# The first weight's scale in front of the first rows, and four pieces decoded without order edges

## The chip, the cores and the metric

The kernel runs on one core of a Trainium2 chip. The metric is device time in microseconds (us) of one execution. Five engines run their own instruction queues and meet at semaphores: PE (TensorE, matrix products), DVE (VectorE), ACT (ScalarE), POOL (GpSimd) and SP (SyncE, which here only starts DMA transfers).

## What is computed

Eight batches of an approximate attention (landmarks, with six Newton steps for an inverse) over q, k, v of 8 heads x 576 tokens x 64, then a two-dimensional Fourier mix, a normalisation and a feed-forward of two matrices:

```python
X = np.fft.fft(np.fft.fft(x, axis=1), axis=2)
u = x + np.real(X)
un = (u - mu) / np.sqrt(var + 1e-06)
ch = np.maximum(un @ w_ch1, 0.0) @ w_ch2
return u + ch
```

x is the attention's output, 8 x 576 rows of 512. `w_ch1` is 512 x 2048 and `w_ch2` 2048 x 512, both float64. The feed-forward is most of the arithmetic.

## The kernel before

All matrix products that matter run as three float16 products of high and low halves (`mm3`). Work is written as Python threads, which a small planner interleaves: `attention`/`tokens`, `landmarks`, `values`, `mix` and `norm` for one batch after the other, `weights` for the two matrices, and `mlp` for the feed-forward. The planner keeps an estimated clock `self.now`, adds estimated durations, and takes at each moment the first thread by priority that isn't waiting. The order in which it emits PE's instructions is PE's order. The order on DVE, ACT and SP is made by the framework's scheduler from the dependencies; the planner adds edges for it (`Timed.emit`): where `A.late` or `V.late` is set to a time, the instruction must stand behind the last instruction on that engine whose estimated start isn't later than that time. Where a loaded piece lands late by the estimate, its decoding so stays behind work that can start earlier.

The weights come as float64 bits in 16 pieces each of 128 x 512 numbers, 0 to 15 for `w_ch1` and 16 to 31 for `w_ch2`. Each piece goes through these steps:

- `prepare`: ACT makes the exponent and upper bits from the high word (`row<-w` or `row<-big` in the trace).
- decoding: the low bits by DVE (even pieces, a TENSOR_SCALAR) or ACT (odd pieces, from a byte), joined by DVE (`w<-row,w`).
- `squares`: PE multiplies the piece with itself into `gram` (four 128 x 128 products, `acc<-w`), for the matrix's norm.
- `scale`, once for each matrix: DVE takes the diagonal (`wd`) and its sum (`wm`), PE adds it over the partitions (product with `ones`), DVE bounds it (`wp_e`), POOL takes the power -1/2 (`wp_r`), DVE writes the scale `wsc`.
- `halve`: ACT and DVE write the scaled piece as high and low float16 halves (`w<-w,wsc`).

No product of the feed-forward can start before its piece is halved. In the kernel before, `squares` lag the decoding by two pieces, and the first scale comes after piece 17.

`norm` normalises finished rows (DVE `row<-u,mv,r`, with POOL's power `r`), and for the first four row tiles transposes them on PE (`at<-ident,row`) and splits them into `unT` (ACT high, DVE low). `mlp` takes two row tiles as a chunk: for each pair of pieces 24 products `h<-unT,w` into one of two PSUM banks, a relu by ACT (high) and DVE (low), and, a little later, 12 products `acc<-w,h` into the chunk's two accumulators, which DVE adds to `u` when the chunk is done (`u<-acc`). Relus of the second chunk's first two pairs go to tiles named `u`.

As long as `self.spare` is there (until the second matrix's first product), the planner fills its own estimated gaps on PE with idle products of `ones16` and `idle`, 128 x 256.

Of the kernel before, what the change touches and what calls it, by code (L numbers as in the profile page):

```python
# [10 lines left out]
F32 = mybir.dt.float32  # L11
# [7 lines left out]
P = 128  # L19
H, S, D, LM, DM, DF = 8, 576, 64, 32, 512, 2048  # L20
NF = DF // P
# [12 lines left out]
AHEAD, PREP, EARLY = 1, 4, 2  # L34
# [124 lines left out]
class Kernel:  # L159
# [80 lines left out]
    def mm(self, out, a, b, start=True, stop=True, share=1.0):  # L240
        self.there[out.name] = self.now
        self.now += share * (1.0e-3 if a.dtype == F32 else 0.42e-3) * math.prod(b.shape[1:])
        self.nc.tensor.matmul(out, a, b, start=start, stop=stop, skip_group_check=True)  # L243

    def tr(self, out, a, ident):
        self.there[out.name] = self.now
        self.now += 0.11
        self.nc.tensor.transpose(out, a, ident)  # L248
# [26 lines left out]
    def weights(self):  # L275
        nc = self.nc
        V, A = self.V, self.A
        whole = self.whole
        slots = [[t[:, OFF + 512 * i : OFF + 512 * i + 512] for i in range(NF)] for t in whole]
        upper = [[t.bitcast(BF16).rearrange("p (m x) -> p m x", x=2)[:, :, 1] for t in ss] for ss in slots]  # L280
        hl = [[t[:, 512 * i : 512 * i + 512].bitcast(F16).rearrange("p (y m) -> p y m", y=2) for i in range(NF)] for t in whole]
        self.w1s = [t.rearrange("p y (c f) -> p y c f", c=KT) for t in hl[0]]
        self.w2s = hl[1]
        sc = self.cp.tile([P, 3], F32, name="wsc")
        pieces = [(w, f) for w in range(2) for f in range(NF)]
        mags = []

        def prepare(i):


            mag = self.row(512)
            top = self.wraw[i].rearrange("p (m x) -> p m x", x=2)[:, :, 1].bitcast(F32)
            A.late = self.raw_there[i]
            A.activation(mag, top, AF.Prelu, scale=2.0**-112, alpha=-(2.0**32))
            mags.append(mag)

        def squares(i):

            w, f = pieces[i]
            for c in range(KT):  # L300
                x = upper[w][f][:, P * c : P * c + P]
                self.mm(self.gram[:, P * w : P * w + P], x, x, i == 0 and c == 0, f == NF - 1 and c == KT - 1)

        es = []

        def scale(w):

            dg, a2 = self.small(P, "wd"), self.small(1, "wm2")
            V.tensor_tensor(dg, self.gram[:, P * w : P * w + P], self.ident, ALU.mult)
            V.tensor_reduce(a2, dg, AX.X, ALU.add)  # L310
            yield self.till(a2, banks=1)
            ps = self.psum()
            self.mm(ps[:, 0:1], self.ones, a2)
            e, r = self.small(1, f"wp{w}_e"), self.small(1, f"wp{w}_r")
            V.tensor_scalar(e, ps[:, 0:1], 2.0**-120, 2.0**126, ALU.max, ALU.min)
            self.G.tensor_tensor(r, e, self.mhalf[:, 0:1], ALU.pow)
            V.tensor_scalar(r.bitcast(I32), r.bitcast(I32), 0x7F800000, None, ALU.bitwise_and)
            V.reciprocal(e, r)
            es.append(e)
            V.tensor_scalar(sc[:, w : w + 1], r, (2.0**12, 2.0**14)[w], None, ALU.mult)  # L320

        def halve():
            w, f = pieces[sum(self.split_w)]
            self.split(hl[w][f][:, 0], hl[w][f][:, 1], slots[w][f], sc[:, w : w + 1])
            self.split_w[w] = f + 1

        for i, (w, f) in enumerate(pieces):
            while len(mags) < min(2 * NF, i + 1 + PREP):
                j = len(mags)
                while len(self.wraw) < min(2 * NF, j + 1 + AHEAD):  # L330
                    self.raw()
                if self.raw_there[j] > self.now:
                    if j > i:
                        break
                    yield self.raw_there[j] - self.now
                    continue
                prepare(j)
            low = self.wraw[i].rearrange("p (m x) -> p m x", x=2)[:, :, 0]
            x, dst = mags[i].bitcast(I32), slots[w][f].bitcast(I32)
            (A if i % 2 else V).late = self.raw_there[i]  # L340
            if i % 2 == 0:
                V.tensor_scalar(dst, low, 29, None, ALU.logical_shift_right)
            else:
                byte = self.wraw[i].bitcast(mybir.dt.uint8).rearrange("p (m x) -> p m x", x=8)[:, :, 3]
                A.activation(dst, byte, AF.Copy, scale=2.0**-5, bias=-0.484375)
            V.scalar_tensor_tensor(dst, x, 3, dst, ALU.logical_shift_left, ALU.bitwise_or)
            if i > 1:
                squares(i - 2)
            self.decoded = i + 1
            if self.decoded == 2 * NF:  # L350
                self.load(1)
            yield max(0.0, max(self.V.free, self.G.free) - self.now - WT)
            if i == NF + 1:
                yield from scale(0)
            for _ in range(PACE if es else 0):
                if self.split_w[0] < NF:
                    halve()
                    yield max(0.0, max(self.V.free, self.G.free) - self.now - WT)
        squares(2 * NF - 2)
        yield 0.0  # L360
        squares(2 * NF - 1)
        yield from scale(1)
        V.tensor_scalar(sc[:, 2:3], es[0], 2.0**-25, es[1], ALU.mult, ALU.mult)
        self.inv2 = sc[:, 2:3]
        while sum(self.split_w) < 2 * NF:
            halve()
            yield max(0.0, max(self.V.free, self.A.free) - self.now - WT)
# [52 lines left out]
    def tokens(self, b, st):  # L420

        nc, mm, mm3, tr, sm, split = self.nc, self.mm, self.mm3, self.tr, self.sm, self.split
        V, A = self.V, self.A
        self.load(b)
# [424 lines left out]
    def norm(self, b, uts):  # L849
        nc, V = self.nc, self.V  # L850
        n = len(uts)
# [29 lines left out]
        for j, ut in enumerate(uts):  # L881
            i = self.ntile
# [7 lines left out]
                )  # L890
            unT = self.unT[-1]
            at = P * (i % TCH)
            if i < 2 * TCH:
                yield self.till(uns[j], banks=1) + (LATER if i >= TCH else 0.0)
                ps = self.psum()
                for c in range(KT):
                    self.tr(ps[:, P * c : P * c + P], uns[j][:, P * c : P * c + P], self.ident)
                self.split(*(unT[:, y, :, at : at + P] for y in range(2)), ps.rearrange("p (c t) -> p c t", c=KT), 1.0)
                self.ready.append(self.now + self.till(unT))
                yield 0.0  # L900
                continue
# [89 lines left out]
    def run(self):  # L991
# [1 line left out]

        self.ntile, self.utiles, self.unT, self.ready = 0, [], [], []
        self.ulive, self.ufree, self.first_done, self.seconds, self.folded = 0, [], 0, 0, -1
        self.split_w, self.decoded = [0, 0], 0
        self.threads = []
        self.spawn(self.attention(), 1)
        self.spawn(self.weights(), 2)
# [85 lines left out]
```

## Time and profile before

| | us |
|---|---|
| median of 3 runs | 994.53 |
| lowest, highest | 993.15, 995.64 |
| the profiled execution | 993.68 |
| its span, first to last instruction | 991.9 |
| PE busy | 955.5 |
| DVE busy | 593.3 |
| ACT busy | 319.4 |
| POOL busy | 119.0 |

The profiled execution is 1.8 us longer than its span. Busy time of PE counts idle products too. In the views a tile's name stands without its buffer number, and as most DVE and ACT instructions go through one helper (L138), groups are told apart by their tiles. A wait is put down to the engine whose semaphore came last.

### The profile page before, as it was taken

The numbers are of one execution on the slowest core, as the hardware profiler recorded it, in microseconds if no ns is written. First come the engines' busy times: TensorE is split into PE (matmuls) and PEld (weight loads), VectorE is DVE, ScalarE is ACT, GpSimd is POOL, SyncE is SP. The second block draws the span as 40 slices with busy tenths as digits, with TensorE's granted clock in tenths as the row PEclk, the third lists the DMA queues.
The fourth block names the chain that finished last, engine by engine and source line by source line (L and its number), as shares of the span: only waits on it lengthen the run. The fifth ranks groups of instructions, "written<-read, shape, count | busy, mean of one in ns | idle before, by whom it ended". The sixth has DMA issues, their size and how long they took to land.

```text
span 991.9 us, 20749 instructions
## 1 busy us (share of the span) xinstructions
PE 955.5 (96%) x8700; PEld 664.2 (67%) x8700; DVE 593.3 (60%) x1593; ACT 319.4 (32%) x652; POOL 119.0 (12%) x124
## 2 busy tenths in 40 slices
PE   6869999899999999999999999999999999999998
PEld 4648656667666777676666776676766777666665
DVE  7989797796467635396467736784634835141111
ACT  5559653243214322143214322432213412120110
POOL 0000000023021301032012301150110401010000
PEclk8889999999999999999999999999999999999999
DMA  9854204135121511025112321134111301020000
GB/s 332 292 212 150 65 2 172 37 59 154 49 44 42 149 55 23 22 58 154 44 44 42 99 104 43 23 61 172 22 33 33 52 1 42 16 40 22 1 22 22
DMA packets 97774, 74.66 MB, mean 75 GB/s; under 512 B 68112, under 2 KB 86544, under 8 KB 97552
## 3 DMA queue, kind: packets, MB, share of 16 engines
q1 hardware_dynamic: 97680, 73.34, 25.6%
q8 instruction: 68, 1.11, 0.5%
q14 instruction: 26, 0.21, 0.1%
HBM read 48.02 MB, written 9.44 MB: 58 GB/s over the span
## 4 chain that ended last, share of the span: by engine, by line
PE 86%; DVE 9%; DMA 2%; ACT 2%; issue 1%; POOL 0%; SPq 0%; DVEq 0%; ACTq 0%; POOLq 0%
PE h L243 36%; PE acc L243 35%; PE at L243 14%; DVE w L138 2%; DVE u L138 1%; DVE lm L138 1%; DVE mid L138 1%; DVE row L138 1%; DMA big<-k_dram 1%; PE at L248 1%; DMA big<-v_dram 1%; ACT w L138 0%; DMA out_dram<-u 0%; ACT row L138 0%; ACT mid L138 0%
## 5 line engine op out<-in xcount | busy, mean ns | idle before, releaser
L243 PE MATMUL h<-unT,w 128*128 128x256 f16 x3456 | 411.2, 273 | 3.8 <-DMA unT<-row 1.7
L243 PEld LDWEIGHTS <-w 128*128 128x128 f16 (+1 forms) x3584 | 344.9, 99 | 79.9 <-DVE w L138 7.3
L243 PE MATMUL acc<-w,h 128*128 128x512 f16 x1632 | 381.6, 380 | 2.7 <-DVE w L138 2.2
L243 PEld LDWEIGHTS <-h 128*128 128x128 f16 x1632 | 157.2, 99 | 162.6 <-issue 6.3
L138 DVE SCALAR_TENSOR_TENSOR h<-h 128x512 f16<-128x512 f32 x136 | 93.6, 688 | 224.8 <-ACT h L138 224.6
L138 ACT ACTIVATE h<-h 128x512 f16<-128x512 f32 x136 | 80.9, 595 | 321.8 <-PE h L243 315.7
L138 POOL TENSOR_TENSOR r<-ve,mhalf 128x2 f32<-128x2 f32 (+1 forms) x20 | 13.3, 667 | 476.6 <-DVE ve L138 472.2
L138 POOL TENSOR_TENSOR mid<-mid 128x640 f16<-128x640 f32 (+2 forms) x36 | 48.7, 1365 | 161.1 <-ACT mid L138 123.7
L138 DVE TENSOR_REDUCE lm<-big 128x32 f32<-128x576 f32 (+1 forms) x48 | 44.5, 940 | 2.8 <-DMA big<-k_dram 2.5
L243 PEld LDWEIGHTS <-big 128*128 128x128 f16 (+1 forms) x864 | 40.1, 103 | 8.1 <-issue 1.9
L138 ACT CAST row<-row 128x512 f16<-128x512 f32 (+1 forms) x40 | 20.8, 552 | 63.9 <-DVE row L138 63.9
L138 POOL TENSOR_TENSOR row<-row 128x512 f16<-128x512 f32 (+1 forms) x33 | 35.4, 1089 | 39.6 <-ACT row L138 37.7
L243 PEld LDWEIGHTS <-mid 64*128 64x128 f16 (+1 forms) x624 | 29.3, 95 | 14.8 <-issue 8.2
L138 DVE SCALAR_TENSOR_TENSOR u<-at,scw,w 128x128 f32<-128x128 f32 (+3 forms) x105 | 33.8, 389 | 5.8 <-PE at L243 4.1
L138 DVE SCALAR_TENSOR_TENSOR u<-acc,wsc,u 128x512 f32<-128x512 f32 x36 | 26.9, 748 | 12.3 <-PE acc L243 12.0
L138 DVE SCALAR_TENSOR_TENSOR w<-at,scw,w 128x262 f32<-128x262 f32 (+1 forms) x42 | 19.1, 485 | 25.2 <-ACT w L138 25.2
L243 PE MATMUL at<-mid,big 128*128 128x262 f16 (+1 forms) x288 | 32.6, 282 | 0.0
L138 DVE TENSOR_TENSOR E<-at,mask 128x256 f32<-128x256 f32 x48 | 20.1, 419 | 17.9 <-PE at L243 17.9
L243 PEld LDWEIGHTS at<-RE,E 128*128 128x128 f32 x192 | 26.6, 194 | 5.0 <-DVE big L138 1.6
L243 PE MATMUL at<-RE,E 128*128 128x64 f32 (+1 forms) x192 | 29.0, 275 | 0.2 <-DVE RE L138 0.2
L138 DVE SCALAR_TENSOR_TENSOR big<-big,aq_r 128x1024 f16<-128x1024 f32 (+1 forms) x32 | 26.8, 868 | 3.5 <-ACT big L138 3.5
L138 DVE TENSOR_TENSOR mid<-mid 128x256 f32<-128x256 f32 (+2 forms) x52 | 28.6, 584 | 0.0
(179 smaller groups left out, 897.8 us busy)
## 6 DMA issues: line engine op xcount, KB each, us to landing
w<-w_dram SPq DMA_DIRECT2D x22, 512.0 KB, 6.8
big<-v_dram SPq DMA_DIRECT2D x16, 640.0 KB, 9.5
big<-q_dram SPq DMA_DIRECT2D x16, 584.0 KB, 6.7
big<-k_dram SPq DMA_DIRECT2D x16, 576.0 KB, 5.4
out_dram<-u SPq DMA_DIRECT2D x36, 256.0 KB, 2.0
big<-w_dram SPq DMA_DIRECT2D x10, 512.0 KB, 6.5
t<-t_dram SPq DMA_DIRECT2D x1, 1048.0 KB, 10.7
unT<-row SPq DMA_TRANSPOSE x64, 2.4
```

What stands on the lines that cost most here:

```text
L138: ins = call(out, *args, **kw)
L243: self.nc.tensor.matmul(out, a, b, start=start, stop=stop, skip_group_check=True)
L248: self.nc.tensor.transpose(out, a, ident)
```

## The change

`squares(14)`, `squares(15)` and `scale(0)` are now emitted right behind the decoding of piece 15. 24 idle products (`warm`) stand in front of `squares(15)` and 8 behind the scale's product with `ones`; that product now uses one of `mlp`'s two banks (`h`). `norm` holds its transposes until this product has been emitted (`self.scaled`). As soon as `es` is filled, the halving of the first matrix runs beside the decoding of the second, so it begins two pieces earlier. For pieces 28 to 31 `late` is 0, so that no order edge is added.

```diff
--- before.py
+++ after.py
@@ -242,6 +242,10 @@
         self.now += share * (1.0e-3 if a.dtype == F32 else 0.42e-3) * math.prod(b.shape[1:])
         self.nc.tensor.matmul(out, a, b, start=start, stop=stop, skip_group_check=True)
 
+    def warm(self, n):
+        for _ in range(n):
+            self.nc.tensor.matmul(self.spare[:, 0:256], self.ones16, self.idle, start=True, stop=True, skip_group_check=True)
+
     def tr(self, out, a, ident):
         self.there[out.name] = self.now
         self.now += 0.11
@@ -290,13 +294,15 @@
 
             mag = self.row(512)
             top = self.wraw[i].rearrange("p (m x) -> p m x", x=2)[:, :, 1].bitcast(F32)
-            A.late = self.raw_there[i]
+            A.late = self.raw_there[i] if i < 2 * NF - PREP else 0.0
             A.activation(mag, top, AF.Prelu, scale=2.0**-112, alpha=-(2.0**32))
             mags.append(mag)
 
         def squares(i):
 
             w, f = pieces[i]
+            if i == NF - 1:
+                self.warm(24)
             for c in range(KT):
                 x = upper[w][f][:, P * c : P * c + P]
                 self.mm(self.gram[:, P * w : P * w + P], x, x, i == 0 and c == 0, f == NF - 1 and c == KT - 1)
@@ -308,9 +314,12 @@
             dg, a2 = self.small(P, "wd"), self.small(1, "wm2")
             V.tensor_tensor(dg, self.gram[:, P * w : P * w + P], self.ident, ALU.mult)
             V.tensor_reduce(a2, dg, AX.X, ALU.add)
-            yield self.till(a2, banks=1)
-            ps = self.psum()
+            yield self.till(a2, banks=1) if w else max(0.0, self.there[a2.name] - self.now)
+            ps = self.psum() if w else self.ps_h.tile([P, 512], F32, name="h")
             self.mm(ps[:, 0:1], self.ones, a2)
+            if w == 0:
+                self.warm(8)
+            self.scaled = True
             e, r = self.small(1, f"wp{w}_e"), self.small(1, f"wp{w}_r")
             V.tensor_scalar(e, ps[:, 0:1], 2.0**-120, 2.0**126, ALU.max, ALU.min)
             self.G.tensor_tensor(r, e, self.mhalf[:, 0:1], ALU.pow)
@@ -337,20 +346,23 @@
                 prepare(j)
             low = self.wraw[i].rearrange("p (m x) -> p m x", x=2)[:, :, 0]
             x, dst = mags[i].bitcast(I32), slots[w][f].bitcast(I32)
-            (A if i % 2 else V).late = self.raw_there[i]
+            (A if i % 2 else V).late = self.raw_there[i] if i < 2 * NF - PREP else 0.0
             if i % 2 == 0:
                 V.tensor_scalar(dst, low, 29, None, ALU.logical_shift_right)
             else:
                 byte = self.wraw[i].bitcast(mybir.dt.uint8).rearrange("p (m x) -> p m x", x=8)[:, :, 3]
                 A.activation(dst, byte, AF.Copy, scale=2.0**-5, bias=-0.484375)
             V.scalar_tensor_tensor(dst, x, 3, dst, ALU.logical_shift_left, ALU.bitwise_or)
-            if i > 1:
+            if i > 1 and not NF <= i < NF + 2:
                 squares(i - 2)
             self.decoded = i + 1
             if self.decoded == 2 * NF:
                 self.load(1)
             yield max(0.0, max(self.V.free, self.G.free) - self.now - WT)
-            if i == NF + 1:
+            if i == NF - 1:
+                squares(NF - 2)
+                yield 0.0
+                squares(NF - 1)
                 yield from scale(0)
             for _ in range(PACE if es else 0):
                 if self.split_w[0] < NF:
@@ -890,6 +902,8 @@
                 )
             unT = self.unT[-1]
             at = P * (i % TCH)
+            while not self.scaled:
+                yield 0.1
             if i < 2 * TCH:
                 yield self.till(uns[j], banks=1) + (LATER if i >= TCH else 0.0)
                 ps = self.psum()
@@ -993,7 +1007,7 @@
 
         self.ntile, self.utiles, self.unT, self.ready = 0, [], [], []
         self.ulive, self.ufree, self.first_done, self.seconds, self.folded = 0, [], 0, 0, -1
-        self.split_w, self.decoded = [0, 0], 0
+        self.split_w, self.decoded, self.scaled = [0, 0], 0, False
         self.threads = []
         self.spawn(self.attention(), 1)
         self.spawn(self.weights(), 2)
```

The planner's clock changes with it, and so does the order of everything behind. PE has 26 idle products more in all (156 instead of 130 of that shape) and the same other products; their order is the same before this place and again, with few differences, from the end of the third batch on.

On PE, at the first weight's scale: `acc_109` are squares, `acc_108` the idle products, `wm` the scale's sum. Before:

```order
L243 MATMUL at<-mid,big 128x262
L243 LDWEIGHTS ones_102
L243 MATMUL acc_108<-idle,ones_102 128x256
L243 LDWEIGHTS ones_102
L243 MATMUL acc_108<-idle,ones_102 128x256
L243 MATMUL at<-wm_1022,ones 128x1
L243 LDWEIGHTS mid
L243 MATMUL at<-Wx,mid 128x4x32
```

And now:

```order
L243 MATMUL acc_109<-w_73 128x128
L243 LDWEIGHTS ones_102
L243 MATMUL acc_108<-idle,ones_102 128x256
L243 LDWEIGHTS ones_102
L243 MATMUL acc_108<-idle,ones_102 128x256
L243 MATMUL h<-wm_999,ones 128x1
L247 LDWEIGHTS ones_102
L247 MATMUL acc_108<-idle,ones_102 128x256
```

Before, the scale's product stood behind the eight transposes of the first rows and the twelve products `at<-mid,big` of the next tile; now it stands behind the squares, and the seven other idle products, the transposes and those twelve products follow it. The 24 idle products stand ahead of the four squares whose last is this piece's first row.

On DVE, at the end of the decoding (`w_74<-row,w_74` joins a piece of the second matrix, `u<-h,u` is the relu of the second chunk's first pairs, `wd` begins the second scale). Before:

```order
L138 TENSOR_SCALAR w_74<-big 128x512
L138 SCALAR_TENSOR_TENSOR w_74<-row,w_74 128x512
L138 SCALAR_TENSOR_TENSOR h<-h 128x512
L138 SCALAR_TENSOR_TENSOR u<-h,u 128x512
L138 SCALAR_TENSOR_TENSOR w_74<-row,w_74 128x512
L138 TENSOR_TENSOR wd<-acc_109,ident 128x128
```

And now:

```order
L138 SCALAR_TENSOR_TENSOR u<-at,scw,row 64x128 x2
L138 SCALAR_TENSOR_TENSOR h<-h 128x512
L138 SCALAR_TENSOR_TENSOR w_74<-row,w_74 128x512
L138 TENSOR_SCALAR w_74<-big 128x512
L138 SCALAR_TENSOR_TENSOR w_74<-row,w_74 128x512 x2
L138 SCALAR_TENSOR_TENSOR u<-h,u 128x512 x2
L138 TENSOR_TENSOR wd<-acc_109,ident 128x128
```

The last pieces are joined ahead of both relus, and the second relu, which stood behind the second scale, is ahead of it. ACT's order moved in the same way. The writes `u<-at` of the first batch's third tile stand right ahead of the relu `h<-h`; before, they stood ten rows higher.

On DVE, in the second batch (`mid<-at,mid` and `row<-at,row` split the transposes, the `mid<-mid` are the folds, `u<-acc` adds a finished accumulator). Before:

```order
L138 SCALAR_TENSOR_TENSOR u<-acc_1671,wsc,u 128x512
L138 RECIPROCAL asum<-asum 128x16
L138 TENSOR_REDUCE asum<-row 128x4
L138 SCALAR_TENSOR_TENSOR u<-acc_1672,wsc,u 128x512
L138 TENSOR_SCALAR asum<-asum 128x4
L138 TENSOR_TENSOR E<-at,mask 128x256
```

And now, the first `u<-acc` being some 13 rows higher:

```order
L138 TENSOR_TENSOR E<-at,mask 128x256
L138 TENSOR_TENSOR mid<-mid 128x256 x2
L138 TENSOR_TENSOR mid<-mid 128x512
L138 TENSOR_TENSOR RE<-RE,at 128x2x32
L138 TENSOR_TENSOR mid<-mid 128x512
L138 SCALAR_TENSOR_TENSOR u<-acc_1694,wsc,u 128x512
```

The second `u<-acc` moved from ahead of the splits to behind the last fold. On PE, 84 products `acc` now stand ahead of the second batch's transposes `at<-ident,mid` of its attention weights, where 99 stood before; behind these transposes follow the first chunk's last products and 24 products of the second chunk, whose sixth to twelfth go to the accumulator that this `u<-acc` empties.

## Rows read from the trace of the kernel before

**Rows 1.** The page's first part, PE's and the other engines' busy time, share of the span and instructions.

```profile
PE 955.5 (96%) x8700; PEld 664.2 (67%) x8700; DVE 593.3 (60%) x1593; ACT 319.4 (32%) x652; POOL 119.0 (12%) x124
```

**Rows 2.** Busy time by stage (windows). After the stretch's bounds in us stand its length, then busy time and instructions of PE, PE's weight loads, DVE, ACT and POOL, then PE's granted clock (1.00 is full speed, 2.4 GHz), the share of the DMA engines and GB/s.

```profile
62.69:82.07 19.38, 15.63 (x123) 12.57 (x123) 14.68 (x41) 11.64 (x23) 1.96 (x3) 0.74 0.25 84
71.47:82.07 10.60, 9.34 (x79) 7.57 (x75) 8.59 (x25) 9.42 (x19) 0.70 (x1) 0.84 0.17 51
82.07:105.38 23.31, 22.49 (x237) 19.86 (x235) 23.20 (x43) 19.65 (x34) 0.00 (x0) 1.00 0.59 194
105.38:111.42 6.04, 5.28 (x55) 4.66 (x54) 2.44 (x8) 2.31 (x4) 0.55 (x1) 1.00 0.13 42
112.77:153.68 40.91, 37.03 (x368) 20.64 (x366) 36.83 (x104) 22.87 (x47) 2.49 (x3) 0.96 0.06 18
153.68:210.00 56.32, 53.31 (x494) 36.17 (x493) 43.12 (x115) 18.04 (x37) 2.11 (x5) 1.00 0.32 97
260.00:992.00 732.00, 726.47 (x6383) 499.84 (x6381) 382.46 (x1017) 189.63 (x389) 98.48 (x97) 1.00 0.19 50
```

**Rows 3.** PE's timeline, first weight's last squares to the first products of the feed-forward. Columns: start and length in us, engine, line, operation, output<-inputs, shape, count, and in brackets the idle time before it and who ended it.

```profile
59.14 0.27 PE L243 MATMUL acc<-idle,ones 128*128 128x256 bf16 x1
62.18 0.40 PE L243 MATMUL acc<-w 128*128 128x128 bf16 x4 [2.77 <-DVE w L138]
...
64.84 1.94 PE L248 MATMUL at<-ident,row 128*128 128x128 f32 x8 [2.15 <-DVE row L138]
66.57 2.83 PE L243 MATMUL at<-mid,big 128*128 128x262 f16 x12
...
69.62 0.43 PE L243 MATMUL at<-wm,ones 128*128 128x1 f32 x2
...
72.42 0.39 PE L243 MATMUL h<-unT,w 128*128 128x256 f16 x2 [0.84 <-ACT w L138]
...
77.53 1.36 PE L243 MATMUL acc<-idle,ones 128*128 128x256 bf16 x11
78.73 1.47 PE L243 MATMUL h<-unT,w 128*128 128x256 f16 x12
```

**Rows 4.** The same window view as in rows 2, single microseconds; the column behind the engines is the granted clock.

```profile
63.00:64.00 1.00, 0.00 (x0) 0.00 (x0) 0.97 (x5) 0.00 (x0) 0.39 (x1) 0.63 0.38 61
69.00:70.00 1.00, 1.00 (x7) 0.86 (x6) 0.00 (x0) 0.48 (x1) 0.00 (x0) 0.50 0.00 0
```

**Rows 5.** Timelines of DVE and POOL, the first weight's scale and the two pairs of normalised rows (columns as in rows 3).

```profile
63.57 0.28 DVE L138 TENSOR_REDUCE wm<-wd 128x1 f32<-128x128 f32 x1
...
64.14 1.00 DVE L138 TENSOR_SCALAR row<-u,mv,r 128x512 f32<-128x512 f32 x2
...
70.08 0.16 DVE L138 TENSOR_SCALAR wp_e<-at 128x1 f32<-128x1 f32 x1 [1.94 <-PE at L243]
...
70.32 0.56 POOL L138 TENSOR_TENSOR wp_r<-wp_e,mhalf 128x1 f32<-128x1 f32 x1 [6.93 <-DVE wp_e L138]
...
71.47 0.14 DVE L138 TENSOR_SCALAR wsc<-wp_r 128x1 f32<-128x1 f32 x1
...
82.07 1.00 DVE L138 TENSOR_SCALAR row<-u,mv,r 128x512 f32<-128x512 f32 x2
```

**Rows 6.** Timelines of ACT, DVE and PE: ACT's first copy for `unT`, and the end of the decoding.

```profile
65.96 0.60 ACT L138 ACTIVATE unT<-at 128x512 f16<-128x512 f32 x1 [5.00 <-PE at L248]
...
105.96 0.60 ACT L138 ACTIVATE u<-h 128x512 f16<-128x512 f32 x1 [2.72 <-PE h L243]
...
106.45 0.67 ACT L138 ACTIVATE row<-big 128x512 f32<-128x512 f32 x1
...
106.59 0.69 DVE L138 SCALAR_TENSOR_TENSOR u<-h,u 128x512 f16<-128x512 f32 x1 [1.12 <-ACT u L138]
...
107.71 0.69 DVE L138 SCALAR_TENSOR_TENSOR w<-row,w 128x512 int32<-128x512 int32 x1 [0.43 <-ACT w L138]
...
108.46 0.41 PE L243 MATMUL acc<-w 128*128 128x128 bf16 x4 [0.77 <-DVE w L138]
```

**Rows 7.** Timelines of DVE and PE behind the second weight's scale: its `wsc`, the second matrix's first products, and PE's waits up to 210 us.

```profile
111.42 0.13 DVE L138 TENSOR_SCALAR wsc<-wp_r 128x1 f32<-128x1 f32 x1
...
112.77 10.91 PE L243 MATMUL acc<-w,mid 128*128 128x512 f16 x48
...
126.78 3.59 PE L243 MATMUL acc<-w,h 128*128 128x512 f16 x11 [2.23 <-DVE w L138]
...
150.47 0.81 PE L243 MATMUL acc<-w,u 128*128 128x512 f16 x3 [1.37 <-DVE u L138]
...
150.63 0.73 DVE L138 SCALAR_TENSOR_TENSOR u<-acc,wsc,u 128x512 f32<-128x512 f32 x1
...
153.79 1.46 PE L243 MATMUL acc<-w,u 128*128 128x512 f16 x6
...
158.56 0.69 DVE L138 TENSOR_TENSOR mid<-mid 128x512 f16<-128x512 f32 x1
...
187.29 0.49 PE L243 MATMUL at<-Wx,mid 64*128 64x128 f16 x11 [0.76 <-DVE w L138]
...
192.33 2.03 PE L243 MATMUL h<-unT,w 128*128 128x256 f16 x17 [1.75 <-DMA unT<-row]
...
207.28 1.46 PE L243 MATMUL acc<-w,h 128*128 128x512 f16 x6 [0.50 <-DVE u L138]
```

## The prediction

> **What bounds the kernel now.** I read the page's busy line first, then busy time by stage, then PE's timeline where it stands still, then the queues of DVE and ACT there. PE is busy 96% of the span [rows 1], and from 260 us on 726.5 of 732 us [rows 2]: nothing can be won there. The change sits where PE waits. In 62.7 to 82.1 us PE works 15.6 of 19.4 us and its granted clock averages 0.74; in 82.1 to 105.4 us DVE works 23.2 of 23.3 us, so that stretch is DVE's; from 112.8 to 153.7 us PE stands still for 3.9 of 40.9 us [rows 2]. PE waits 2.77 us for piece 15, then 2.15 us for the first rows [rows 3]; behind these gaps the clock goes to 0.5, half speed, and is there still at 69 to 70 us [rows 4]. The first product of the feed-forward starts at 72.42 [rows 3], because the scale `wsc` comes at 71.47 [rows 5], although its sum `wm` was there at 63.85 [rows 5]: PE's product with it is queued behind eight transposes and twelve products and ends at 70.05 [rows 3].
>
> **The idle products.** Eleven run from 77.53 to 78.73, 0.109 us each [rows 3]. 24 take 2.6 us and lie in the gap from 59.4 to 62.18 [rows 3]: nothing unless they start over 0.1 us later, and then that much. Eight more, 0.9 us, lie between the scale's product (about 64.1) and the first transposes (65.0). With PE busy from 59 to 66 I take the clock to stay full; at half speed the eight transposes and twelve products took from 64.84 to 69.40 [rows 3], 4.6 us, at full speed I take half of it. If the clock falls all the same, that half, 2.3 us, isn't won (the third rival).
>
> **The scale.** `wm` ends at 63.85; the product takes 0.3, `wp_e` follows at 64.2, POOL's power 0.24 us later for 0.56 us [rows 5], and `wsc` is there at 65.6, 5.9 us earlier. The two row normalisations stand behind `wp_e` and slip by 0.1 to 0.4 us. ACT has no work until 65.96 [rows 6] and takes the first split in that hole; its two copies for `unT` come behind it, and DVE's second part of `unT` ends at about 68.3, near to where it did. So `unT` becomes what is late, and the first products start at 68.3, 4.1 us earlier.
>
> **Splitting and decoding.** PE cannot keep the 4.1 us, since each pair of pieces must be split by DVE first. DVE is idle for 4.7 us in 62.69 to 82.07, when the second pair of rows is normalised [rows 2, 5]. Counting along its new queue I find waits of 1.6 us (0.45 for POOL's power of the rows, 0.15 for PE's product, 0.7 for ACT's first split, 0.3 for POOL again), and one relu of 0.6 us more stands ahead of these rows: 4.7 - 1.6 - 0.6 = 2.5 us earlier, and 0.6 us less left to do, 3.1 together. From there the queue is full, as it was. At the end the last piece's decoding stands in ACT's queue behind the relu `u<-h`, for which ACT waits 2.72 us; DVE then waits 1.12 for that relu and 0.43 for the piece [rows 6]. In the new order decoding is in front of both relus: 1.55 us of waiting and a relu of 0.6 go, and the last piece's decoding starts 3.1 + 1.55 + 0.6 = 5.2 us earlier (102.5 instead of 107.71 [rows 6]). PE does not follow quite: the relu that frees the ninth tile's bank is behind the third tile's three `u` writes in DVE's queue, about 100.4, so that the last squares come at 104.5 (108.46 before [rows 6]). Both have twelve products between these and the scale's product: the second `wsc` comes at 107.6 instead of 111.42 [rows 7], a lead of 3.8 us. Bounds: 5.2 if PE follows DVE, 1.0 if DVE's early waits stay and only the 1.55 us at the end go, shared with PE.
>
> **From the second scale on.** The 264 products of the first eleven tiles are done in both before the second matrix starts (at 112.77 [rows 7]); before, 24 covered the wait for its scale, now six do. It then waits for DVE's splitting, as before (2.23 us at 126.78 [rows 7]), and the lead is kept. But the new PE order brings the second batch's transposes with 84 `acc` products done instead of 99: 15 products of 0.227 us (48 took 10.91 [rows 7]), 3.4 us of cover, are behind them. PE now goes straight from the `kbd` products through two Newton steps into four transposes, whose operand POOL has yet to make: I count 2.3, 1.0 and 1.5 us of waiting. Then the next chunk's second accumulator `acc_2245` needs DVE's `u<-acc_1694`, and that stands on DVE behind the folds of the second batch. The folds ended at 159.25 [rows 7]; 159.25 - 3.8 (lead) - 0.6 (a relu done earlier) - 0.7 (this `u`, now behind) + 0.5 (new waiting) is 154.65 for their end, and with the 0.73 of such a write [rows 7] the accumulator is free at 155.4; PE is there at 152.4. At that point PE has done what it had done at 153.90 before [rows 7] (288 products of the first matrix in both; three `acc` products fewer, 0.7 us, and two Newton steps more, about as much). So the lead of 3.8 has become a loss of 1.5 us.
>
> What says that `u<-acc_1694` can't go ahead when its operand is there (about 150.7) is a row: `row<-big` starts on ACT at 106.45, right behind the relu that waited for PE, though it needs nothing of PE [rows 6]. The Trainium skill says so too (TensorE: Matmul & The Clock Gate, section "Architectural detail: the array is 16× 32×32, not 1× 128×128"): ScalarE and VectorE are strict queues, and PE alone pulls weight loads ahead. By that rule the wait stays, as in my sum; the trace agrees by the 106.45 above. If it could pass, PE would lose nothing there, which is the faster rival's time below.
>
> **Clock and later waits.** Behind the 2.23 us gap eleven products took 3.59 us [rows 7] instead of 2.5: 1.1 us. The new gap of 3.0 us gets the same 1.1. Further on PE waited 0.76, 1.75 and 0.50 us [rows 7]. The first comes from DVE's order at the second tile, which stays. The other two are rows and accumulators of a batch that now runs ahead of PE: I let 2.25 us go. Both are unsure: 0 to 3.3 for the clock, 0 to 3.0 for the waits.
>
> **Sum.** +1.5 + 1.1 - 2.25 = +0.35 us on the profiled execution's 993.68 (span 991.9 and 1.8 around it): 994.0. The median of the runs shown is 994.53, within a spread of 2.5; I make no correction for it.
>
> **Rivals.**
> - Faster: the lead survives. If DVE reaches `u<-acc_1694` by 152.4, or the plan's waits at the transposes cover it, PE never stands at `acc_2245`: equal work 1.5 us earlier than 153.90, no clock cost, 2.25 us of later waits gone, 3.75 us less: 989.9; with the later lead growing to the 5.2, 988.5. For it: DVE has another 4 us of slack in 112.8 to 153.7 [rows 2]. Against: it needs a lead of 7.6 at the folds, twice what I count.
> - Slower: the early stage doesn't close up. Fewer order edges let ACT take a preparation before its transfer or its row buffer is there, and in an in-order queue splits and relus stand behind it; DVE, full from 82 on [rows 2], can't catch up. With a lead of 1.0 the loss at `acc_2245` is 1.5 + 2.8 = 4.3, plus 1.1, less 2.25: +3.15, 996.8. It decides from a lead under 1.2 at the second scale. For it: ACT too is busy 9.4 of 10.6 us in 71.47 to 82.07 [rows 2], and its first preparations of the second matrix now come after the first splits. Against: ACT's long waits here were for PE [rows 6], and none that I read was for a transfer.
> - The idle products don't hold the clock: half speed lasts to 70 us as before. The transposes, then `unT`, come 0.6 us later, the first products of the feed-forward 2 us later, but DVE's splits set the pace there; the lead falls by about 1: 995.0, no change.
>
> **Chances.** Forecast 0.43, clock rival 0.05, faster 0.31, slower 0.21. A measurement of this kernel can tell about 0.3% (3 us) from no change, so faster by more than that has 0.31, within it 0.48, slower 0.21. The likeliest case alone spans 992 to 996.5. The range over all is 988.8 to 997.3: it takes in most of the faster rival and the slower one at its price, with half of the 0.85 us to the median.
>
> **What will show it.** Granted clock 1.0 from 60 to 68 us; `wsc` near 65.6; first `h` product near 68.3; second `wsc` near 107.6; then PE waits of 1 to 3 us between 140 and 156 us, the longest at an `acc` product for DVE's `u`; no wait of 1.75 us for `unT` near 190. The forecast is wrong if the second `wsc` comes before 106 or after 110, if PE has no wait for `u<-acc` there, or if the second batch's transposes don't make PE wait; then the lead is kept or was never there.

## The result and the profile after

The changed kernel takes 999.93 us (median of 4 runs, 999.77 to 1000.89), the kernel before 994.24 beside it. The ratio is 1.0057, with a 95% interval of 1.0042 to 1.0072: slower, by 5.7 us, and outside the predicted range of 988.8 to 997.3. The profiled execution took 1000.89 us (span 999.1). The page's first part hardly differs from [rows 1]: 1.4 us more of PE, 26 products more (the idle ones), so the rest of the 7.2 us of span is PE standing still.

```profile
PE 956.9 (96%) x8726; PEld 664.5 (67%) x8726; DVE 594.9 (60%) x1593; ACT 319.3 (32%) x652; POOL 118.6 (12%) x124
```

PE is at the first weight's last squares 1.86 us later than before (64.04 against 62.18 [rows 3]), though its order is the same up to the 24 idle products. That start scatters from profile to profile (last section). So all that follows is counted from these squares; "lead" is by how much an event stands nearer behind them than before. The stretch ends with a row that stands in every kernel, the fourth batch's landmark products (the expectations below miscount and call it the fifth). In the profile of the kernel before, PE's timeline there (columns as in rows 3):

```profile
310.29 1.23 PE L243 MATMUL at<-big,lm 64*32 64x288 f32 x16 [0.78 <-DVE u L138]
```

PE's timeline of the changed kernel, its first weight's scale and the end of the stretch:

```profile
61.01 2.78 PE L247 MATMUL acc<-idle,ones 128*128 128x256 bf16 x24
64.04 0.40 PE L243 MATMUL acc<-w 128*128 128x128 bf16 x4 [0.25 <-DVE w L138]
...
65.71 0.38 PE L243 MATMUL h<-wm,ones 128*128 128x1 f32 x2 [1.04 <-DVE wm L138]
...
66.89 1.08 PE L252 MATMUL at<-ident,row 128*128 128x128 f32 x8
67.81 1.52 PE L243 MATMUL at<-mid,big 128*128 128x262 f16 x12
...
69.49 0.27 PE L243 MATMUL h<-unT,w 128*128 128x256 f16 x1
70.46 0.71 PE L243 MATMUL h<-unT,w 128*128 128x256 f16 x5 [0.70 <-DVE unT L138]
...
317.44 1.23 PE L243 MATMUL at<-big,lm 64*32 64x288 f32 x16 [0.92 <-DVE u L138]
```

The stretch lasted 310.29 - 62.18 = 248.11 us before and 317.44 - 64.04 = 253.40 after: 5.29 us more. Behind it come 681.6 us in one as in the other (991.9 - 310.29 and 999.1 - 317.44). The whole loss is in the stretch, and not in its first part: the idle products fill the gap of 2.77 us [rows 3], the transposes take 1.08 us instead of 1.94 and the twelve products 1.52 instead of 2.83, and the first `h` product starts 5.45 us behind the squares instead of 10.24. The granted clock, 0.50 before at 69 to 70 us [rows 4], is 1.00 there now (same view):

```profile
69.00:70.00 1.00, 0.76 (x7) 0.52 (x6) 1.00 (x3) 1.00 (x3) 0.00 (x0) 1.00 0.00 0
```

DVE's timeline there (both scales, the second rows, the last decoding):

```profile
67.53 0.13 DVE L138 TENSOR_SCALAR wsc<-wp_r 128x1 f32<-128x1 f32 x1
...
81.93 0.99 DVE L138 TENSOR_SCALAR row<-u,mv,r 128x512 f32<-128x512 f32 x2
...
103.90 1.28 DVE L138 SCALAR_TENSOR_TENSOR w<-row,w 128x512 int32<-128x512 int32 x2
...
110.93 0.13 DVE L138 TENSOR_SCALAR wsc<-wp_r 128x1 f32<-128x1 f32 x1
```

Behind the squares these stand at 3.49 (first scale, 9.29 before), 17.89 (second rows, 19.89), 39.86 for the last two pieces (45.53 for the last) and 46.89 (second scale, 49.24): a lead of 5.8 us, then 2.0, over 5, and at the second scale 2.35. PE from 83 us to the second matrix's first products shows who set that last number:

```profile
83.64 0.61 PE L243 MATMUL h<-unT,w 128*128 128x256 f16 x4 [0.76 <-DVE w L138]
...
107.74 0.62 PE L243 MATMUL acc<-w 128*128 128x128 bf16 x8
108.20 1.47 PE L243 MATMUL h<-unT,w 128*128 128x256 f16 x12
109.51 0.28 PE L243 MATMUL at<-wm,ones 128*128 128x1 f32 x2
...
111.87 0.38 PE L243 MATMUL acc<-w,mid 128*128 128x512 f16 x1 [1.40 <-ACT w L138]
112.65 7.64 PE L243 MATMUL acc<-w,mid 128*128 128x512 f16 x26 [0.41 <-DVE w L138]
...
125.88 3.18 PE L243 MATMUL acc<-w,h 128*128 128x512 f16 x14 [0.19 <-DVE w L138]
```

From 83.64 to 110 PE has no gap with a releaser. The last squares start 3.84 us behind the row of the last two decodings (0.75 behind the last one's before [rows 6]): DVE had decoded, PE was not there yet. The new order has 258 `h` products ahead of the second scale's product, the old one 240 (the expectations below say 259, 253 and 265: they count the first scale's own product, which also writes to an `h` bank). Then the second batch, PE and DVE:

```profile
146.73 0.66 PE L243 MATMUL at<-RE,E 128*128 128x64 f32 x4 [2.30 <-DVE RE L138]
148.12 1.12 PE L252 MATMUL at<-ident,mid 128*128 128x128 f32 x4 [0.73 <-POOL mid L138]
149.03 2.45 PE L243 MATMUL acc<-w,h 128*128 128x512 f16 x6
...
153.74 0.33 PE L252 MATMUL at<-ident,row 128*128 128x128 f32 x1 [1.43 <-POOL row L138]
153.91 1.46 PE L243 MATMUL acc<-w,h 128*128 128x512 f16 x6
...
159.87 4.04 PE L243 MATMUL acc<-w,u 128*128 128x512 f16 x18 [2.82 <-DVE u L138]
```

```profile
158.46 0.69 DVE L138 TENSOR_TENSOR mid<-mid 128x512 f16<-128x512 f32 x1
159.07 0.74 DVE L138 SCALAR_TENSOR_TENSOR u<-acc,wsc,u 128x512 f32<-128x512 f32 x1
```

Four waits, 7.28 us in all; before there was one of 1.37 [rows 7]. `u<-acc` runs right behind the last fold, though its accumulator was complete at 155.37 (153.91 + 1.46). The work done at 159.87, 95.83 us behind the squares, was done before at about 153.90 (the prediction's count, from the row at 153.79 [rows 7]), 91.72 behind them: 4.11 us are lost here. Two more new waits come in the third batch, in place of 1.75 and 0.50 us [rows 7]:

```profile
189.60 0.49 PE L243 MATMUL at<-Wx,mid 64*128 64x128 f16 x11 [1.01 <-DVE w L138]
...
217.31 0.16 PE L243 MATMUL at<-kb,ones 128*128 128x1 bf16 x1 [1.68 <-ACT mid L138]
...
220.26 0.46 PE L243 MATMUL at<-nrm,ones_bd 128*128 128x128 f32 x2 [1.45 <-DVE nrm L138]
```

### The profile page after: what moved, and what is told of

Its sections match the earlier page's. It is cut to its first block, busy times and chain, and to the rows that moved or that the text cites. A ratio compares the mean times of both kernels' runs of the same rounds, so it can differ in the third digit from the quotient of the medians.

```text
span 999.1 us, 20803 instructions
## 1 busy us (share of the span) xinstructions
PE 956.9 (96%) x8726; PEld 664.5 (67%) x8726; DVE 594.9 (60%) x1593; ACT 319.3 (32%) x652; POOL 118.6 (12%) x124
## 4 chain that ended last, share of the span: by engine, by line
PE 77%; DVE 3%; DMA 0%; ACT 0%; issue 0%; POOL 0%; POOLq 0%; DVEq 0%; ACTq 0%
PE acc L243 33%; PE h L243 33%; PE at L243 11%; DVE u L138 1%; DVE lm L138 1%; DMA out_dram<-u 0%; DVE h L138 0%; DVE big L138 0%; DVE row L138 0%; DVE bn L138 0%; DVE cmx L138 0%; DVE nrm L138 0%; POOL r L138 0%; ACT h L138 0%; ACT big L138 0%
```

## The experiments

Theory: PE's new order brings the second batch with too little accumulation in front of it ("cover"), and the waits there eat a small but real lead. Rivals: the missing order edges do the harm; the lead itself is what decides; or the waits only move. "Stretch" is always from the start of the first weight's last squares to the marked row of `at<-big,lm`, in the profiled execution. "Cover" is the number of `acc` products that PE's order has ahead of the second batch's first and second transposes of exponentials (before 99 and 105, after 84 and 90). Each stretch is that of one profiled execution, and the clock has a part in it. In all five profiles with a cover of 84 and 90 (after, e1, e3, e6, e7) the granted clock falls to 0.50 between 145 and 157 us; in the nine others it doesn't.

**e1: the scale part alone.** The changed kernel with the edges of before.

```diff
-            A.late = self.raw_there[i] if i < 2 * NF - PREP else 0.0
+            A.late = self.raw_there[i]
```

(and the same at the decoding's line)

> The change without its second part: the last four pieces keep their order edges, the scale and the idle products are as in the changed kernel, and so is PE's order. Theory (the loss is made by PE's order at the second batch, and the missing edges only bring the end of decoding forward): second wsc 1 to 2 us later than in the changed kernel, the waits at the second batch as large or larger, 1000 to 1002 us. Rival (the missing edges do the harm, because ACT takes preparations too early): the loss goes, 994 to 996 us.

Ratio to before 1.0089 (1.0065 to 1.0113); stretch 254.26. The rival falls, the edges are not the loss. But the theory missed too: the second scale came at 46.86, where it was with the edges gone, though the last decoding ended later. PE, second matrix:

```profile
112.47 10.52 PE L243 MATMUL acc<-w,mid 128*128 128x512 f16 x47 [0.41 <-DVE w L138]
...
125.69 3.18 PE L243 MATMUL acc<-w,h 128*128 128x512 f16 x14 [1.84 <-DVE w L138]
```

The wait of 1.84 us was 0.19 in the changed kernel, but it costs nothing: it ends 61.82 us behind the squares here and 61.84 there. PE only came earlier, at 0.224 us a product; in the changed kernel 26 of them took 7.64, 0.294 each, at a granted clock of 0.50 from 113.6 to 116.8 us.

**e2: the edges part alone.** Those two lines of the change put into the kernel before, nothing else.

> The kernel before with the second part of the change alone: the last four pieces without order edges; PE's order is that of before. Theory: the end of decoding loses its 1.55 us of waiting, the second wsc comes 1.0 to 1.5 us earlier, the second batch's transposes keep their 99 products of cover, and the time is 0.5 to 1.5 us shorter than before: 993 us. Rival (the missing edges do the harm): 997 us or more.

Ratio 0.9985 (0.9971 to 0.9999), stretch 246.30, 1.81 less than before; second scale at 48.30, 0.94 earlier. That is a little under the theory's 1.0. Part of the rest is the clock: the gap of 2.23 us is still there, but the eleven products behind it took 2.53 us where they took 3.59 [rows 7].

```profile
129.14 2.53 PE L243 MATMUL acc<-w,h 128*128 128x512 f16 x11 [2.23 <-DVE w L138]
```

**e3: the folds behind the write.** In the second batch's plan, ahead of the folds:

```diff
+        while b == 1 and self.seconds < NF // 2:
+            yield 0.3
         F1 = [self.mid()[:, 0:512] for _ in range(2)]
```

> The changed kernel, the second batch's folds planned behind the first chunk's last accumulator, so that DVE writes u<-acc of the second accumulator behind one fold instead of seven. Theory: the wait of 2.8 us at the second chunk's second accumulator falls under 0.8 us, and 1.5 to 2.5 us of the time go: 997.5 to 998.5 us. Rival (the products that take the folds then wait instead, or the lag behind the write is made up later anyway): no change, 999.5 to 1000.5 us.

Ratio 1.0062 (1.0036 to 1.0088); stretch 253.20, and 683.26 us behind it instead of 681.6. The wait of 2.82 us is gone and nothing is won: the rival was right about the time. PE's timeline shows where it went:

```profile
147.51 2.77 PE L243 MATMUL acc<-w,h 128*128 128x512 f16 x6
...
153.16 2.77 PE L243 MATMUL acc<-w,h 128*128 128x512 f16 x6
...
315.74 1.54 PE L243 MATMUL at<-big,lm 64*32 64x288 f32 x16 [2.80 <-DVE u L138]
```

Both groups of six products ran at half speed (in the changed kernel the second took 1.46), and at the end of the stretch PE waits 2.80 us instead of 0.92; behind that wait the granted clock is 0.50 again, and the 1.6 us behind the stretch go there (e12 is the only other profile with both). The first three of the four waits are still there (2.30, 0.73 and 1.02). Taking away the last one alone wins nothing.

**e4: more cover.**

```diff
-HOLD = 2.5
+HOLD = 4
```

> The changed kernel with the hold of the second batch at 4.0 us instead of 2.5: the planner puts 108 to 117 acc products ahead of the second batch's transposes instead of 84 to 90, nothing else is meant to change up to there. Theory (too little cover behind the second scale): the waits for RE, mid, row and u there, 7.2 us in the changed kernel, fall under 3, and the time falls by 3 to 5 us: 995 to 997 us. Rival (the loss was made before the second scale, or the waits only move to the later attention products): 999 to 1001 us.

991.83 us, ratio 0.9982 (0.9969 to 0.9996), better than the theory's 995 to 997 us; stretch 244.58, 8.8 us less than the changed kernel and 3.5 less than before. The second scale is at 46.89 as in the changed kernel; only what comes behind it differs. PE's timeline of the same work:

```profile
149.03 0.60 PE L252 MATMUL at<-ident,mid 128*128 128x128 f32 x4
...
153.03 0.27 PE L252 MATMUL at<-ident,row 128*128 128x128 f32 x1
...
154.83 0.63 PE L243 MATMUL at<-RE,E 128*128 128x64 f32 x4 [0.88 <-DVE RE L138]
...
157.91 2.75 PE L243 MATMUL acc<-w,unT 128*128 128x512 f16 x12
...
308.15 1.23 PE L243 MATMUL at<-big,lm 64*32 64x288 f32 x16 [0.83 <-DVE u L138]
```

Of 7.28 us of waiting 0.88 are left. DVE wrote both accumulators long before the batch's folds:

```profile
137.30 0.74 DVE L138 SCALAR_TENSOR_TENSOR u<-acc,wsc,u 128x512 f32<-128x512 f32 x1
...
139.06 0.74 DVE L138 SCALAR_TENSOR_TENSOR u<-acc,wsc,u 128x512 f32<-128x512 f32 x1
```

**e5: the same hold in the kernel before.** The same line, 2.5 to 4.0.

> The kernel before with nothing but the hold of the second batch at 4.0 us: 108 to 111 acc products ahead of its transposes instead of 99 to 105. Theory (the first scale's lead of 2.4 us is real and is kept once there is cover): the hold alone gives at most the 1.4 us of the wait for u, so 992.5 to 994 us, and the stretch from the first weight's last squares to the fifth batch's landmark products lasts 246.7 to 248.1 us (248.11 in the kernel before, 244.58 in the changed kernel with this hold). Rival (the hold makes the whole gain, the change adds nothing): 244 to 245.5 us in that stretch, 990 to 991.5 us.

Ratio 0.9993 (0.9981 to 1.0005), stretch 248.81. The hold alone wins nothing, even loses 0.7 of the stretch, a little outside what the theory allowed; the rival falls clearly. Lead and cover together (e4) are worth 4.2 us against this. Part of that is the third batch, where this kernel has a wait of 1.69 us and e4 has none (see the later waits below). e12 has the same cover and the same wait there with the early scale: its second scale comes 2.84 us earlier and its stretch is 3.20 us shorter, so with cover the lead is kept.

**e6: no idle products.** The two calls `self.warm(24)` and `self.warm(8)` taken out of the changed kernel.

> The changed kernel without the 24 and the 8 idle products. Theory (they hold the clock): granted clock 0.5 behind the wait for the last piece, the eight transposes and twelve products take 3.5 to 4.7 us instead of 2.6, the first wsc stays within 0.3 us but the first h product comes 1 to 2 us later, and the second wsc 0.3 to 1.0 us later; time 0.5 to 1.5 us longer than the changed kernel, ratio to before about 1.007. Rival (the clock or the early products don't matter, since PE's products ahead of the second scale and DVE's splits set it): second wsc within 0.1 us, ratio as for the changed kernel, 1.0057.

Ratio 1.0096 (1.0081 to 1.0111); stretch 254.05, second scale at 47.66, so 0.77 us later: the theory. The ratio is above the theory's 1.007; the profiled run began late, with the squares at 66.93. First the granted clock (windows, columns as in rows 2), then PE's timeline:

```profile
70.00:71.00 1.00, 1.00 (x5) 1.00 (x6) 0.65 (x4) 0.00 (x0) 0.32 (x1) 0.50 0.00 0
```

```profile
69.97 1.94 PE L252 MATMUL at<-ident,row 128*128 128x128 f32 x8 [0.80 <-DVE row L138]
71.70 2.03 PE L243 MATMUL at<-mid,big 128*128 128x262 f16 x12
```

**e7: the second scale ahead of six `h` products.** The planner's lead time for the last four pieces goes from 0.4 to 2 us.

```diff
-            yield max(0.0, max(self.V.free, self.G.free) - self.now - WT)
+            yield max(0.0, max(self.V.free, self.G.free) - self.now - (WT if i < 2 * NF - PREP else 2.0))
```

> The changed kernel with the planner told that DVE is ready sooner at the last four pieces, which puts the second scale's product behind 253 h products instead of 259; the second batch's order stays (84 and 90 acc products ahead of its transposes). Theory (the second scale is set by PE's products ahead of it, 0.109 us each, not by the last decode): second wsc 46.2 us behind the first weight's last squares instead of 46.89, the last decode where it was (39.9). Rival (it is set by DVE's decode): 46.9, nothing moves. The time changes by less than can be told, 0 to -0.7 us against the changed kernel.

The last decoding stays at 39.84, the second scale moves to 46.44: 0.45 of the 0.65 us that six products take. PE's queue sets it. For the other 0.2, `wd` now starts at 111.09 right behind a relu on DVE, which had waited 1.93 us for ACT's half of it, and so for PE's products. Stretch 252.80, 0.6 less. Ratio 1.0079 (1.0064 to 1.0094): the profiled run began late (66.83 at the squares); that the others did is not shown.

**e8: the rows not held.** Without `while not self.scaled: yield 0.1` in `norm`.

> The changed kernel without the wait that holds the first rows' transposes behind the scale's product: transposes and twelve products go ahead of that product again, 265 h products stand ahead of the second scale instead of 259, and the planner puts 102 to 111 acc products ahead of the second batch's transposes instead of 84 to 90. Theory (the cover at the second batch decides, not the lead at the second scale): second wsc 0.7 to 2 us later than in the changed kernel (47.6 to 48.9 us behind the first weight's last squares), yet the fifth batch's landmark products start 249 to 251 us behind those squares instead of 253.4: 995 to 997 us. Rival (the lead decides): 254 us or more, 1000 us or more.

The second scale comes at 49.16: the lead is gone (49.24 before). Yet the stretch is 248.50, 4.9 us less than in the changed kernel (both a little outside the theory's bounds), ratio 1.0025 (1.0006 to 1.0044), with runs from 993.70 to 1002.37. Its cover is 102 and 111. Part of the 4.9 is the clock, which stays at 1.00 through this stretch; what the changed kernel lost by it in the second batch is by estimate 1.5 us (six products 2.45 us instead of 1.46, four transposes 1.12 instead of 0.61). So it is the cover more than the lead that parts the changed kernel from the one before.

**e9 to e12: what is worth something once there is cover.** The changed kernel with the hold at 4.0, and: the edges back (e9, the diff of e1); no idle products (e10, as e6); the hold at 5.0 (e11); the diff of e7 (e12).

> The changed kernel with the hold at 4.0 us and with the order edges of the last four pieces back. Theory (the missing edges are worth the wait of 1.84 us for the second weight's splits that came back without them, about 0.9 us in all): the stretch from the first weight's last squares to the fifth batch's landmark products lasts 245.2 to 245.8 us (244.58 with the hold and no edges), second wsc at 46.9. Rival (with cover, the edges are worth nothing): 244.4 to 244.8 us. Second rival (without cover they were hidden, now they show in full): 246.4 us or more.

> The changed kernel with the hold at 4.0 us and without the 24 and the 8 idle products. Theory (they are worth the 0.77 us by which the second scale comes earlier, whatever follows): second wsc 47.5 to 47.8 us behind the first weight's last squares, the stretch lasts 245.2 to 245.7 us. Rival (with cover the lead is lost in a later wait): 244.4 to 244.8 us.

> The changed kernel with the hold at 5.0 us: 111 to 120 acc products ahead of the second batch's transposes. Theory (cover is now enough, the lead is all there is): within 0.6 us of the hold at 4.0, the stretch 244.0 to 245.2 us, since only the waits of 0.91 us for nrm and 0.88 us for RE are left there. Rival (more cover brings more): under 244.0 us. Second rival (the second batch comes too late for the third): 246 us or more.

> The changed kernel with the hold at 4.0 us and the second scale's product behind 253 h products instead of 259. Theory (a lead won at the second scale is kept when there is cover): the second wsc 0.45 us earlier (46.44) and the stretch 243.9 to 244.4 us. Rival (the 3 to 6 products less ahead of the transposes bring a wait back): 245 us or more.

| | second scale | cover | stretch | ratio to before (95%) |
|---|---|---|---|---|
| e4 | 46.89 | 108, 117 | 244.58 | 0.9982 (0.9969 to 0.9996) |
| e9 | 46.89 | 108, 117 | 245.00 | 0.9969 (0.9958 to 0.9981) |
| e10 | 48.45 | 108, 117 | 246.34 | 0.9995 (0.9982 to 1.0008) |
| e11 | 46.89 | 111, 120 | 245.14 | 0.9981 (0.9968 to 0.9995) |
| e12 | 46.43 | 108, 111 | 245.61 | 0.9993 (0.9978 to 1.0007) |

e9: the edges are worth 0.42 us of the stretch, between theory and first rival; in time e4 and e9 can't be told apart. e10: the idle products are worth 1.76 us, more than expected, because the scale was 1.56 us later this time: the granted clock stayed at 0.50 longer than in e6 (the twelve products took 2.83 us, in e6 2.03). e11 is the theory: enough cover is enough. e12 is the rival in its number: 0.46 us won at the scale and 1.03 lost in the stretch, with waits of 1.68 in the third batch and 2.27 at the end (behind which half speed costs another 1.6 us). That the six acc products fewer ahead of the second transposes bring them is not shown. e9, at 991.28 us (991.10 to 991.74), beats both kernels: the scale part of the change, the old edges, the hold at 4.0.

## Why the prediction was wrong

- **Clock and idle products: right.** Full speed from 60 to 68 us, as said, and beyond; e6 prices them at 0.7 us of the stretch, e10 at 1.76 (the third rival put it at about 1).
- **The early scale: right.** Predicted 65.6, that is 3.4 behind the squares, measured 3.49; first `h` product predicted 6.1 behind, measured 5.45, with `unT` the late one, as said.
- **Rows and decoding: right.** Second rows 17.4 behind the squares by the prediction, 17.89 measured; last decoding 40.3 against the second half of a row of two that starts at 39.86 and takes 1.28.
- **The lead at the second scale: the first step that failed.** "The relu that frees the ninth tile's bank ... so that the last squares come at 104.5" put them 42.3 behind; the row of eight whose second half they are starts at 43.70, and the lead was 2.35 us, not 3.8. The step looked only at who releases a bank and never counted PE's own queue: 18 more `h` products ahead of the scale's product, 2.0 us at the 0.109 of an idle product, which has their shape [rows 3]. The prediction names them itself ("before, 24 covered the wait for its scale, now six do") without adding their time. e7 (six fewer, 0.45 us earlier) and e1 (decoding later, scale unmoved) show it. By its own sign, a second `wsc` after 110 us, the forecast is wrong too (110.93), but only by the late start: counted from the squares it is 62.18 + 46.89 = 109.07.
- **The second batch: the waits right, place by place, the clock right by luck.** Predicted waits of 2.3, 1.0, 1.5 and 3.0 us, measured 2.30, 0.73, 1.43 and 2.82, the last for `u<-acc_1694` behind the folds. With the true lead the step gives 1.5 + (3.8 - 2.35) + 1.1 for the clock = 4.05 us; 4.11 were lost. But the 1.1 stood behind the longest wait, and there the products ran at full speed (18 in 4.04 us). About as much was lost ahead of it, where six products took 2.45 us instead of 1.46 and four transposes 1.12 instead of 0.61; that this is what made the folds and the `u` behind them late was read from the trace and not tried. The `u` at 159.07 agrees with the strict queues that the Trainium skill states for VectorE (TensorE: Matmul & The Clock Gate, section "Architectural detail: the array is 16× 32×32, not 1× 128×128"). e3 corrects the reading, not the number: with this wait away the time stays; e4, which gives cover back, leaves 0.88 of the 7.28 us.
- **The later waits: the second step that failed.** "I let 2.25 us go" was half right: the waits of 1.75 and 0.50 went. But 1.68 and 1.45 came in the third batch, and 0.76 became 1.01: from 159.87 on the changed kernel loses another 5.29 - 4.11 = 1.18 us. In e4 the old wait of 1.69 for `unT` is back and the two new ones are gone. The wait of 1.68 goes with PE's order in the third batch: the seven profiles that have it (1.68 to 2.10; after, e1, e3, e5, e6, e7, e12) have 462 `h` products ahead of its `at<-kb,ones`, the seven without it (0.12 at most) 480, with 204 `acc` products in all of them. So cover is short there too, by 18 products or 2.0 us, and e5 and e12 show that it can be so with a cover of 108 and 111 in the second batch. It was not tried alone.

The sum closes, as it must: +0.35 forecast, 4.11 less the predicted 1.5 + 1.1, so 1.51, of which the lead is 1.45, and 1.18 + 2.25 = 3.43 from the later waits, 5.29 in all. So the larger error is the later waits, which were let go without a count of what would stand in front of the third batch. Of the rivals, "slower" had its price (996.8) too low and its mechanism wrong: it needed a lead under 1.2 from preparations that came too early, and e2 shows that the missing edges do no harm. "Faster" named the condition that e4 then met, the plan's waits covering the transposes; the lead of 7.6 that it asks for instead is 6.8 by the prediction's own terms (159.25 - 0.6 - 0.7 + 0.5 + 0.73 - 152.4).

## What to carry to other kernels

A lead won early is worth only what the plan behind it lets through: where an order is fixed by an estimate, count the covering work in front of every hand-over between engines before and after, and set the hold together with the change. When you ask what sets a moment, count the queue of every engine that has work ahead of it, also of the one that seems to be waiting. Here, removing the last of a row of waits won nothing, and giving back their common cover did. Ask of each wait where it ends, and not how long it is: where another engine sets the end, a longer wait only says that this one came earlier (1.84 against 0.19 us, e1).

## What was not expected of the hardware

The length of a wait alone does not tell whether the clock falls. In the changed kernel PE's waits of 2.30 and 0.73 us, with little work between, were followed by half speed: six products took 2.45 us. The longer wait of 2.82 us was not: eighteen products behind it took 4.04 us, 0.224 each. Windows of the changed kernel, the granted clock behind the engines:

```profile
148.00:150.00 2.00, 1.88 (x7) 1.27 (x8) 1.11 (x6) 0.88 (x3) 0.88 (x2) 0.50 0.00 0
...
160.00:162.00 2.00, 2.00 (x10) 0.88 (x9) 0.00 (x0) 0.00 (x0) 0.00 (x0) 1.00 0.62 168
```

The start scatters by nearly as much as the change moves: the last squares stood at 62.13 to 66.93 us in the fourteen profiles, one of each kernel, and up to the squares of the piece before, all fourteen have the same order on PE, DVE and POOL. One piece of it, PE's timeline of the kernel before and then of the changed kernel, in the same order:

```profile
38.15 2.50 PE L243 MATMUL acc<-idle,ones 128*128 128x256 bf16 x16
40.83 0.66 PE L243 MATMUL at<-RE,E 128*128 128x64 f32 x4 [0.18 <-DVE RE L138]
...
41.55 0.99 PE L243 MATMUL at<-t,mid 128*128 128x160 f16 x12
```

```profile
37.55 1.91 PE L243 MATMUL acc<-idle,ones 128*128 128x256 bf16 x16
41.15 0.66 PE L243 MATMUL at<-RE,E 128*128 128x64 f32 x4 [1.69 <-DVE RE L138]
...
41.94 1.80 PE L243 MATMUL at<-t,mid 128*128 128x160 f16 x12
```

The idle products ran faster, so the gap behind them was longer, and the products after it ran at half speed. But neither does this gap decide. In e8 it is as long, and the products behind it run at full speed (e10 is like it):

```profile
36.86 1.91 PE L243 MATMUL acc<-idle,ones 128*128 128x256 bf16 x16
40.46 0.66 PE L243 MATMUL at<-RE,E 128*128 128x64 f32 x4 [1.69 <-DVE RE L138]
...
41.19 0.99 PE L243 MATMUL at<-t,mid 128*128 128x160 f16 x12
```

What starts such a run on one foot or the other was not tried.
